# Moving where the matmul operands start in SBUF, modulo 512 bytes, in an attention and MLP kernel

## The chip, the cores and the metric

The kernel runs on one core of a Trainium2 chip. The metric is the device time of one execution in microseconds (us); lower is better. The five engines named here are TensorE (PE, with its weight loads shown apart as PEld), VectorE (DVE), ScalarE (ACT), GpSimd (POOL) and SyncE (SP), which issues most transfers.

## What is computed

The input is q, k and v of shape 4 x 8 x 576 x 64 and two weight matrices, w_in (512 x 2048) and w_out (2048 x 512). Attention is the sum of a global part on tokens averaged in fours and a local part in which a token sees the three before and behind it. Its output, 2304 tokens of 512 features, goes through a two-layer network with a softplus between:

```python
def _attn_ref(q, k, v):                      # B, H, S, D = 4, 8, 576, 64; factor = 4
    out_d = sm_attn(q_d, k_d, v_d)           # q_d, k_d, v_d: means over 4 tokens
    out_up = np.repeat(out_d, factor, axis=2)
    mask = np.abs(pos[:, None] - pos[None, :]) < factor
    ...
    return out_up + np.matmul(attn, v)       # attn: softmax of the masked scores

def _moe_ref(x, w_in, w_out):                # x: 2304 x 512
    h = x @ w_in
    g = np.maximum(h, 0.0) + np.log1p(np.exp(-np.abs(h)))
    return (g @ w_out).astype(np.float32)
```

## The kernel before

**The network's two layers.** Tokens are taken in five groups (`NG`): four of 512 and a last one of 256, the short group. The hidden features are taken in 16 slices of 128 (`NF`). For each group g and slice f, `layer1` multiplies the tokens by 128 columns of w_in, softplus follows, and `layer2` multiplies the result by 128 rows of w_out and adds into four accumulators in PSUM, one for each 128 output features. All of this runs with activations as the moving operand, 512 or 256 columns wide, and weights as the stationary operand, 128 x 128.

**Halves.** Every float32 operand is held as two float32r tiles, a high half and a low half: `xh`, `xl` for the tokens, `gh`, `gl` for the softplus, and `wi..h`, `wi..l`, `wo..h`, `wo..l` for the weights. A product is three matmuls: high by high, low by high, high by low. So a block, one `layer1` or one `layer2` of one f, has 4 x 3 = 12 matmuls. They are recorded on L732 (layer 1) and L797 (layer 2), and they alternate in both lines between the high tile, the low tile and the high tile of the activations.

**Weights in two sets.** The weights of f = 0 to 7 are in the tiles of set 0 (wi0h, wi0l, wo0h, wo0l), those of f = 8 to 15 in set 1 (wi1..., wo1...). Below, "first half" and "second half" of w_in or w_out mean these sets. Set 1 is made in a pool (`late`) that takes the place of the tiles of the first batch's attention (`start`).

**Softplus.** Behind a block of layer 1, ScalarE takes Abs (L752), Exp (L755) and Ln (L756), VectorE adds max(h, 0) (L761), GpSimd makes gh (L770) and VectorE makes gl (L778). `layer2` of a slice runs two slices later than its `layer1` (`LAG`), so in the steady state TensorE runs a block of layer 1 of f and a block of layer 2 of f - 2 by turns.

**Attention.** There are 16 units (a batch and two heads each). The first four run ahead of the network, the other twelve are spread between the blocks of the first groups. A unit cuts the stream of blocks at three places: its scores (L418, L481), its transposes (L550) and its products with v (L574, L582). A unit's output goes to `x`, and ScalarE and VectorE make the halves `xh`, `xl` of it (L617, L623, and `fill` at L645, L650).

**Order.** `Plan` orders all instructions when the program is built, from costs and due times written in the code; no time of the chip enters. Its costs don't depend on addresses.

**Places.** A tile pool lays tiles out in a partition in the order in which they are first made, each behind the last. The one pool `pool` holds everything but the first batch's attention and weight set 1. The places that follow from it are given with the change. The matmul of layer 1, whose operands' places change:

```python
nc.tensor.matmul(
    h.t[:, :n], w[:, cc, fs], x.t[:, cc, :n],
    start=(cc == 0 and k == 0), stop=(cc == NCC - 1 and k == 2),
)
```

Of the kernel before, what the change touches and what calls it, by code (L numbers as in the profile page):

```python
# [10 lines left out]
F32 = mybir.dt.float32  # L11
F32R = mybir.dt.float32r
# [5 lines left out]
ALU = mybir.AluOpType  # L18
# [7 lines left out]
P = 128  # L26
# [3 lines left out]
NCC = DM // P  # L30
# [12 lines left out]
GN = 512  # L43
NG = -(-NT // GN)
FB = NF // 2
SCALE = 1.0 / float(D) ** 0.5
NEG = -1000000000.0
EPS = 1e-09
LAG = 2
ON_PE = ()  # L50
TOP_POOL = lambda which, f: False
V_PE = ()
# [13 lines left out]
def cut(b):  # L66
    return (b + 1) * GN - b * S


def gn(g):  # L70
    return min(GN, NT - g * GN)


FIFO = ("h", "t", "gh", "gl", "xh", "xl", "x")
# [177 lines left out]
def kernel(  # L252
# [8 lines left out]
    out: bass.AP,  # L261
):
    nc = tc.nc
    pool = ctx.enter_context(tc.tile_pool(name="pool", bufs=1))
    psum = ctx.enter_context(tc.tile_pool(name="psum", bufs=1, space=PSUM))
    late = ctx.enter_context(ExitStack())
# [6 lines left out]
    op = plan.op  # L273
# [10 lines left out]

    def new_weights(p):
        i = len(wi)
        wi.append([p.tile([P, NCC, FB * P], F32R, name=f"wi{i}{n}") for n in "hl"])
        wo.append([p.tile([P, FB, DM], F32R, name=f"wo{i}{n}") for n in "hl"])

    new_weights(pool)  # L290
    first = start.__enter__()

    def to_late():
        if len(wi) == 1:
            start.__exit__(None, None, None)
            new_weights(late.enter_context(tc.tile_pool(name="late", bufs=1)))

    def buf(tag, shape, bufs, name, dt=F32, home=None):
        home = home or pool
        assert caps.setdefault(tag, bufs) == bufs  # L300
        return Buf(tag, lambda: home.tile(shape, dt, tag=tag, bufs=bufs, name=name))

    def bank(tag, name):
        return Buf(tag, lambda: psum.tile([P, 512], F32, tag=tag, bufs=BANKS[tag], name=name))
# [5 lines left out]

    xh, xl, xs = {}, {}, {}
    for g in range(NG):
        xh[g] = buf("xh", [P, NCC, GN], 2, f"xh{g}", F32R)
        xl[g] = buf("xl", [P, NCC, GN], 2, f"xl{g}", F32R)
    for b in range(B):
        xs[b] = buf("x", [P, NPAIR, S], 1, f"x{b}")
    xparts = {g: [set() for _ in range(NCC)] for g in range(NG)}
# [6 lines left out]
    def attention(u, s):  # L324
# [23 lines left out]
        scale = SCALE / (FACTOR * FACTOR)  # L348
        if u in ON_PE:
            sums = bank("acc", f"sums{u}")  # L350
# [283 lines left out]
    def fill(b):  # L634
        g = b + 1
        n = S - cut(b)
        cost = 0.2 + NCC * n / 960.0
        prio = 2 * NF * b + 1
        src = [(xs[b], p) for p in range(NPAIR)]
        for p in range(NCC):  # L640
            xparts[g][p].add("tail")
        keys = [(p, "tail") for p in range(NCC)]
        op(
            "ACT", cost, prio,
            lambda: nc.scalar.copy(xh[g].t[:, :, :n], xs[b].t[:, :, cut(b) :]),  # L645
            r=src, w=[(xh[g], x) for x in keys],
        )
        op(
            "DVE", cost, prio + 0.5,
            lambda: nc.vector.tensor_tensor(  # L650
                out=xl[g].t[:, :, :n], in0=xs[b].t[:, :, cut(b) :],
                in1=xh[g].t[:, :, :n].bitcast(F32), op=ALU.subtract,
            ),
            r=src + [(xh[g], x) for x in keys], w=[(xl[g], x) for x in keys], port=True,
        )
# [64 lines left out]
    gt, acc = {}, {}  # L720

    def layer1(g, f):
        i = g * NF + f
        h = bank("acc" if g == 0 and 2 <= f < NSPLIT else "h", f"h{g}_{f}")
        n = gn(g)
        fs = slice(f % FB * P, (f % FB + 1) * P)

        def mm(ccs):
            wih, wil = wi[f // FB]
            for cc in ccs:  # L730
                for k, (w, x) in enumerate(((wih, xh[g]), (wih, xl[g]), (wil, xh[g]))):
                    nc.tensor.matmul(  # L732
                        h.t[:, :n], w[:, cc, fs], x.t[:, cc, :n],
                        start=(cc == 0 and k == 0), stop=(cc == NCC - 1 and k == 2),
                    )

        split = [[cc] for cc in range(NCC)] if f < (2 if g else NSPLIT) else [list(range(NCC))]
        for ccs in split:
            xk = [(cc, part) for cc in ccs for part in sorted(xparts[g][cc])]
            op(  # L740
                "PE", 0.23 * 3 * len(ccs) * n / GN, 2 * i + 0.01 * ccs[0], lambda ccs=ccs: mm(ccs),
                r=[("wh", "i", f), ("wl", "i", f)]
                + [(xh[g], k) for k in xk]
                + [(xl[g], k) for k in xk],
                w=[h],
            )
        hh = lambda: h.t[:, :n]
        tt = buf("t", [P, GN], 2, f"t{g}_{f}")
        tv = lambda: tt.t[:, :n]
        c = 0.1 + 0.5 * n / GN  # L750
        pr = 2 * i + 3
        op("ACT", c, pr, lambda: nc.scalar.activation(out=tv(), in_=hh(), func=AF.Abs), r=[h], w=[tt])  # L752

        def expln():
            nc.scalar.activation(out=tv(), in_=tv(), func=AF.Exp, scale=-1.0)  # L755
            nc.scalar.activation(out=tv(), in_=tv(), func=AF.Ln, bias=1.0)  # L756

        op("ACT", 2 * c, pr, expln, w=[tt])
        op(
            "DVE", 0.15 + 0.54 * n / GN, pr,  # L760
            lambda: nc.vector.scalar_tensor_tensor(  # L761
                out=tv(), in0=hh(), scalar=0.0, in1=tv(), op0=ALU.max, op1=ALU.add
            ),
            r=[h], w=[tt],
        )
        gh = buf("gh", [P, GN], 2, f"gh{g}_{f}", F32R)
        gl = buf("gl", [P, GN], 2, f"gl{g}_{f}", F32R)
        op(
            "POOL", 0.1 + 0.75 * n / GN, pr,
            lambda: nc.gpsimd.tensor_scalar(  # L770
                out=gh.t[:, :n], in0=tv(), scalar1=1.0, scalar2=0.0, op0=ALU.mult, op1=ALU.add
            ),
            r=[tt], w=[gh],
        )
        ge = GL_ENG(g)
        op(
            ge, (1.4 if ge == "POOL" else 0.7) * n / GN, pr,
            lambda: eng[ge].tensor_tensor(  # L778
                out=gl.t[:, :n], in0=tv(), in1=gh.t[:, :n].bitcast(F32), op=ALU.subtract
            ),  # L780
            r=[tt, gh], w=[gl], port=True,
        )
        gt[g, f] = (gh, gl)

    def layer2(g, f):
        i = g * NF + f
        n = gn(g)
        if f == 0:
            acc[g] = [bank("acc", f"acc{g}_{k}") for k in range(NCC)]
        gh, gl = gt.pop((g, f))  # L790

        def mm():
            woh, wol = wo[f // FB]
            for m in range(NCC):
                ms = slice(m * P, (m + 1) * P)
                for k, (w, a) in enumerate(((woh, gh), (woh, gl), (wol, gh))):
                    nc.tensor.matmul(  # L797
                        acc[g][m].t[:, :n], w[:, f % FB, ms], a.t[:, :n],
                        start=(f == 0 and k == 0), stop=(f == NF - 1 and k == 2),
                    )  # L800

        op(
            "PE", 0.23 * 12 * n / GN, 2 * i + 2 * LAG + 1, mm,
            r=[gh, gl, ("wh", "o", f), ("wl", "o", f)], w=acc[g],
        )
        if f < NF - 1:
            return
        final = g == NG - 1
        for m in range(NCC):
            o = buf("stage", [P, 2, GN], 4, f"osb{g}_{m}") if m % 2 == 0 else o  # L810
            e = "ACT" if m % 2 == 0 else "DVE"

            def copy(m=m, o=o):
                d = o.t[:, m % 2, :n]
                if final and m == NCC - 1:
                    nc.vector.tensor_copy(d[:, : n // 2], acc[g][m].t[:, : n // 2])
                    nc.scalar.copy(d[:, n // 2 :], acc[g][m].t[:, n // 2 : n])
                elif m % 2 == 0:
                    nc.scalar.copy(d, acc[g][m].t[:, :n])
                else:  # L820
                    nc.vector.tensor_copy(d, acc[g][m].t[:, :n])

            pr = 2 * i + 2 * LAG + 1
            op(e, 0.65, pr, copy, r=[acc[g][m]], w=[(o, m % 2)])
            q = "ACT" if final and m == NCC - 1 else "SP"

            def store(m=m, o=o, q=q):
                eng[q].dma_start(
                    out=out[m * P : (m + 1) * P, g * GN : g * GN + n], in_=o.t[:, m % 2, :n]
                )  # L830

            op(q, 0.1, pr, store, r=[(o, m % 2)], kb=256)
# [7 lines left out]
    for i in range(P // HW):  # L840
        bm = base[i * HW : (i + 1) * HW, :]
        nc.gpsimd.affine_select(
            out=bm, in_=bm, pattern=[[1, HW]], base=0,
# [3 lines left out]
            out=bm, in_=bm, pattern=[[-1, HW]], base=2 * REACH,  # L847
# [20 lines left out]
    for g in range(NG):  # L868
        for f in range(NF):
            layer1(g, f)  # L870
            i = g * NF + f
            if i >= LAG:
                layer2(*divmod(i - LAG, NF))
    for i in range(NG * NF - LAG, NG * NF):
        layer2(*divmod(i, NF))
# [59 lines left out]
```

## Time and profile before

| | before |
|---|---|
| median of 3 runs | 507.99 us (506.65 to 508.0) |
| span of the profiled execution | 506.7 us |
| TensorE busy (matmuls) | 493.6 us, 97% |
| VectorE busy | 269.2 us, 53% |
| ScalarE busy | 245.2 us, 48% |
| GpSimd busy | 92.0 us, 18% |
| granted TensorE clock, mean | 0.997 of full speed |

The span runs from the first to the last instruction of one execution; what lies around it is not in the profile. A matmul's duration in the profile runs from its start to the modelled end of its results, and the next matmul starts before that end. So durations of matmuls overlap, and how fast a stream of them goes is read from start to start: two rows of the timeline some matmuls apart, divided by their number. The timeline gives starts to 0.01 us, so a step is the better known the more matmuls lie between the two rows.

### The profile page before, as it was taken

Reading aid. Unit: us, or ns where it says so; the run is one execution under the profiler, and the core shown is the slowest. Engines: PE = TensorE matmul, PEld = TensorE weight load, DVE = VectorE, ACT = ScalarE, POOL = GpSimd, SP = SyncE. Lnnn points to the kernel's source line nnn. Section 1 sums busy time; section 2 is a strip of 40 time slices with the busy share of each in tenths; the row PEclk is TensorE's granted clock in tenths of the full one; section 3 lists DMA queues with packets and bytes.
Section 4 is the critical chain, followed back from the end, with each engine's and each line's share of the span. In section 5 each row is a group of like instructions: output and inputs, shape, how many; then the busy total and the mean of one; then the engine's idle time right before and its main releaser. Section 6 shows DMA issues by size and latency. Waiting matters only on the chain.

```text
span 506.7 us, 12503 instructions
## 1 busy us (share of the span) xinstructions
PE 493.6 (97%) x5388; PEld 406.3 (80%) x5388; DVE 269.2 (53%) x512; ACT 245.2 (48%) x528; POOL 92.0 (18%) x133
## 2 busy tenths in 40 slices
PE   6799999999999999999999999999999999999996
PEld 4568778888888888888888888888888888889996
DVE  5667998898877646374264636453332222223322
ACT  3457987678556345333344535342442332234342
POOL 5633131131111111020011201120011001001110
PEclk9989999999999999999999999999999999999999
DMA  8924566666614303021014121100020000002001
GB/s 261 329 70 157 183 217 219 226 180 197 215 34 149 87 1 104 9 97 37 19 50 138 49 56 50 34 1 1 0 84 0 1 1 0 1 0 85 1 1 41
DMA packets 15798, 42.86 MB, mean 85 GB/s; under 512 B 1792, under 2 KB 2304, under 8 KB 15744
## 3 DMA queue, kind: packets, MB, share of 16 engines
q1 hardware_dynamic: 15600, 41.94, 25.8%
q8 instruction: 42, 0.69, 0.6%
q10 hardware_dynamic: 144, 0.13, 0.1%
q14 instruction: 12, 0.10, 0.1%
HBM read 37.35 MB, written 4.72 MB: 83 GB/s over the span
## 4 chain that ended last, share of the span: by engine, by line
PE 95%; DMA 2%; DVE 1%; issue 1%; ACT 0%
PE acc L797 40%; PE h L732 38%; PE po L582 5%; PE psc L481 3%; PE psd L418 3%; PE busy L888 2%; PE po L574 2%; PE pdt L550 2%; DMA wri<-in_w_in_dram 1%; DMA qT<-in_qt_dram 1%; DVE qd L381 0%; DVE kd L381 0%; DVE wri L686 0%; PE psc L474 0%; ACT top L679 0%
## 5 line engine op out<-in xcount | busy, mean ns | idle before, releaser
L761 DVE SCALAR_TENSOR_TENSOR t<-h,t 128x512 f32<-128x512 f32 (+1 forms) x80 | 50.8, 634 | 139.7 <-ACT t L756 139.7
L752 ACT ACTIVATE t<-h 128x512 f32<-128x512 f32 (+1 forms) x80 | 44.4, 555 | 160.6 <-PE h L732 147.1
L770 POOL TENSOR_SCALAR gh<-t 128x512 fp32r<-128x512 f32 (+1 forms) x80 | 51.0, 638 | 345.4 <-PE acc L797 206.7
L778 DVE TENSOR_TENSOR gl<-t,gh 128x512 fp32r<-128x512 f32 (+1 forms) x80 | 52.4, 656 | 42.8 <-POOL gh L770 42.8
L732 PE MATMUL h<-xh,wi0h 128*128 128x512 f32 (+1 forms) x160 | 61.1, 382 | 0.7 <-DVE t L761 0.7
L797 PE MATMUL acc<-gh,wo0h 128*128 128x512 f32 (+1 forms) x160 | 60.1, 376 | 0.0
L732 PE MATMUL h<-xh,wi1h 128*128 128x512 f32 (+1 forms) x160 | 60.1, 376 | 0.0
L797 PE MATMUL acc<-gh,wo1h 128*128 128x512 f32 (+1 forms) x160 | 60.1, 375 | 0.0
L732 PE MATMUL h<-xh,wi0l 128*128 128x512 f32 (+1 forms) x160 | 59.5, 372 | 0.0
L797 PE MATMUL acc<-gl,wo1h 128*128 128x512 f32 (+1 forms) x160 | 59.5, 372 | 0.0
L732 PE MATMUL h<-xl,wi0h 128*128 128x512 f32 (+1 forms) x160 | 59.4, 372 | 0.0
L797 PE MATMUL acc<-gh,wo1l 128*128 128x512 f32 (+1 forms) x160 | 59.4, 371 | 0.0
L732 PE MATMUL h<-xh,wi1l 128*128 128x512 f32 (+1 forms) x160 | 59.4, 371 | 0.0
L732 PE MATMUL h<-xl,wi1h 128*128 128x512 f32 (+1 forms) x160 | 59.3, 371 | 0.0
L797 PE MATMUL acc<-gl,wo0h 128*128 128x512 f32 (+1 forms) x160 | 59.1, 369 | 0.0
L797 PE MATMUL acc<-gh,wo0l 128*128 128x512 f32 (+1 forms) x160 | 59.0, 369 | 0.0
L756 ACT ACTIVATE t<-t 128x512 f32<-128x512 f32 (+1 forms) x80 | 47.2, 590 | 2.5
L755 ACT ACTIVATE t<-t 128x512 f32<-128x512 f32 (+1 forms) x80 | 47.2, 590 | 2.3
L732 PEld LDWEIGHTS h<-xh,wi0h 128*128 128x128 f32 x160 | 30.0, 188 | 6.9 <-DVE t L761 1.4
L732 PEld LDWEIGHTS h<-xh,wi0l 128*128 128x128 f32 x160 | 30.0, 188 | 6.0 <-DVE wi0l L711 0.3
L732 PEld LDWEIGHTS h<-xh,wi1l 128*128 128x128 f32 x160 | 30.1, 188 | 5.7
L797 PEld LDWEIGHTS acc<-gh,wo1l 128*128 128x128 f32 x160 | 30.0, 188 | 5.7
(90 smaller groups left out, 765.0 us busy)
## 6 DMA issues: line engine op xcount, KB each, us to landing
wri<-in_w_in_dram SPq DMA_DIRECT2D x16, 511.8 KB, 6.0
wro<-in_w_out_dram SPq DMA_DIRECT2D x16, 511.8 KB, 4.0
vw<-in_vwin_dram SPq DMA_DIRECT2D x16, 384.0 KB
qT<-in_qt_dram SPq DMA_DIRECT2D x16, 292.0 KB, 3.5
kT<-in_kt_dram SPq DMA_DIRECT2D x16, 292.0 KB, 6.5
stage<-in_vrow_dram SPq DMA_DIRECT2D x16, 288.0 KB
out_dram<-osb SPq DMA_DIRECT2D x16, 256.0 KB, 3.0
out_dram<-osb SPq DMA_DIRECT2D x3, 128.0 KB, 1.8
```

Of the source, the lines that this page charges most:

```text
L418: nc.tensor.matmul(pd3()[:, r, :], qb[:, r * RD : (r + 1) * RD], kd.t, start=True, stop=True)
L481: nc.tensor.matmul(pc()[o : o + HW, t, :], q.t[hp, c : c + HW], k.t[hp, c : c + HW], start=not early, stop=not early or t == NTL - 1,)
L550: nc.tensor.transpose(pt.t[:HD, r * RD : (r + 1) * RD], sd.t[:, r, c * HD : (c + 1) * HD], ident[:RD, :RD],)
L582: nc.tensor.matmul(po[h].t[j * D : (j + 1) * D, t * HT : (t + 1) * HT], vw.t[kp, t, :], sT.t[kp, t, :HT], start=True, stop=True,)
L732: nc.tensor.matmul(h.t[:, :n], w[:, cc, fs], x.t[:, cc, :n], start=(cc == 0 and k == 0), stop=(cc == NCC - 1 and k == 2),)
L752: op("ACT", c, pr, lambda: nc.scalar.activation(out=tv(), in_=hh(), func=AF.Abs), r=[h], w=[tt])
L755: nc.scalar.activation(out=tv(), in_=tv(), func=AF.Exp, scale=-1.0)
L756: nc.scalar.activation(out=tv(), in_=tv(), func=AF.Ln, bias=1.0)
L761: lambda: nc.vector.scalar_tensor_tensor(out=tv(), in0=hh(), scalar=0.0, in1=tv(), op0=ALU.max, op1=ALU.add),
L770: lambda: nc.gpsimd.tensor_scalar(out=gh.t[:, :n], in0=tv(), scalar1=1.0, scalar2=0.0, op0=ALU.mult, op1=ALU.add),
L778: lambda: eng[ge].tensor_tensor(out=gl.t[:, :n], in0=tv(), in1=gh.t[:, :n].bitcast(F32), op=ALU.subtract),
L797: nc.tensor.matmul(acc[g][m].t[:, :n], w[:, f % FB, ms], a.t[:, :n], start=(f == 0 and k == 0), stop=(f == NF - 1 and k == 2),)
```

## The change

A new pool, `even`, is opened ahead of `pool`. A pad of 96 float32 is its first tile, and xh, xl, gh and gl are made in it. A pad is also made ahead of each set of weights (32 and 112 float32). The columns of the short group start at column 240 (960 bytes) of their buffers instead of column 0: in `fill`, which writes xh and xl, in the two instructions that write gh and gl, and in the matmuls of both layers (`cols`).

The rows of a tile are multiples of 512 bytes apart in these operands, so one number, the place modulo 512, holds for all slices of a tile:

| start in the partition, modulo 512 bytes | before | after |
|---|---|---|
| xh, xl (moving, layer 1) | 192 | 0 |
| gh, gl (moving, layer 2) | 0 | 0 |
| wi0, wo0 (first half of the weights) | 256 | 256 |
| wi1, wo1 (second half) | 320 | 256 |
| moving columns of the short group, layer 1 | 192 | 448 |
| moving columns of the short group, layer 2 | 0 | 448 |

From the moving tile's start to the weight tile's start, modulo 512, this is:

| distance in bytes, modulo 512 | before | after |
|---|---|---|
| layer 1, first half of w_in | 64 | 256 |
| layer 1, second half | 128 | 256 |
| layer 2, first half of w_out | 256 | 256 |
| layer 2, second half | 320 | 256 |
| short group, all four kinds | 64, 128, 256, 320 | 320 |

In whole addresses, xh, xl, gh and gl move from 107,200 to 156,672 bytes to 1,536 to 42,496, ahead of everything else; weight set 0 moves from 7,936 to 49,408, and set 1 from 162,112 to 163,072. Of the other tiles, ident, mask, the block tile of the later units and the tiles of the weights' upper parts (`top`) change their place modulo 512 by 128 bytes, and so do some small tiles of sums; q, k, v, the staging tiles, t and attention's other tiles keep theirs.

The order of the instructions is the same, row for row, on every engine; only addresses differ.

```diff
--- before.py
+++ after.py
@@ -47,6 +47,9 @@
 NEG = -1000000000.0
 EPS = 1e-09
 LAG = 2
+EVEN_PAD = 96
+ODD_PAD = (32, 112)
+SHORT_AT = 240
 ON_PE = ()
 TOP_POOL = lambda which, f: False
 V_PE = ()
@@ -69,6 +72,11 @@
 
 def gn(g):
     return min(GN, NT - g * GN)
+
+
+def cols(g):
+    o = 0 if gn(g) == GN else SHORT_AT
+    return slice(o, o + gn(g))
 
 
 FIFO = ("h", "t", "gh", "gl", "xh", "xl", "x")
@@ -261,6 +269,8 @@
     out: bass.AP,
 ):
     nc = tc.nc
+    even = ctx.enter_context(tc.tile_pool(name="even", bufs=1))
+    even.tile([P, EVEN_PAD], F32, name="evenpad")
     pool = ctx.enter_context(tc.tile_pool(name="pool", bufs=1))
     psum = ctx.enter_context(tc.tile_pool(name="psum", bufs=1, space=PSUM))
     late = ctx.enter_context(ExitStack())
@@ -284,6 +294,7 @@
 
     def new_weights(p):
         i = len(wi)
+        p.tile([P, ODD_PAD[i]], F32, name=f"oddpad{i}")
         wi.append([p.tile([P, NCC, FB * P], F32R, name=f"wi{i}{n}") for n in "hl"])
         wo.append([p.tile([P, FB, DM], F32R, name=f"wo{i}{n}") for n in "hl"])
 
@@ -310,8 +321,8 @@
 
     xh, xl, xs = {}, {}, {}
     for g in range(NG):
-        xh[g] = buf("xh", [P, NCC, GN], 2, f"xh{g}", F32R)
-        xl[g] = buf("xl", [P, NCC, GN], 2, f"xl{g}", F32R)
+        xh[g] = buf("xh", [P, NCC, GN], 2, f"xh{g}", F32R, even)
+        xl[g] = buf("xl", [P, NCC, GN], 2, f"xl{g}", F32R, even)
     for b in range(B):
         xs[b] = buf("x", [P, NPAIR, S], 1, f"x{b}")
     xparts = {g: [set() for _ in range(NCC)] for g in range(NG)}
@@ -635,6 +646,7 @@
         g = b + 1
         n = S - cut(b)
         cost = 0.2 + NCC * n / 960.0
+        gc = slice(cols(g).start, cols(g).start + n)
         prio = 2 * NF * b + 1
         src = [(xs[b], p) for p in range(NPAIR)]
         for p in range(NCC):
@@ -642,14 +654,14 @@
         keys = [(p, "tail") for p in range(NCC)]
         op(
             "ACT", cost, prio,
-            lambda: nc.scalar.copy(xh[g].t[:, :, :n], xs[b].t[:, :, cut(b) :]),
+            lambda: nc.scalar.copy(xh[g].t[:, :, gc], xs[b].t[:, :, cut(b) :]),
             r=src, w=[(xh[g], x) for x in keys],
         )
         op(
             "DVE", cost, prio + 0.5,
             lambda: nc.vector.tensor_tensor(
-                out=xl[g].t[:, :, :n], in0=xs[b].t[:, :, cut(b) :],
-                in1=xh[g].t[:, :, :n].bitcast(F32), op=ALU.subtract,
+                out=xl[g].t[:, :, gc], in0=xs[b].t[:, :, cut(b) :],
+                in1=xh[g].t[:, :, gc].bitcast(F32), op=ALU.subtract,
             ),
             r=src + [(xh[g], x) for x in keys], w=[(xl[g], x) for x in keys], port=True,
         )
@@ -730,7 +742,7 @@
             for cc in ccs:
                 for k, (w, x) in enumerate(((wih, xh[g]), (wih, xl[g]), (wil, xh[g]))):
                     nc.tensor.matmul(
-                        h.t[:, :n], w[:, cc, fs], x.t[:, cc, :n],
+                        h.t[:, :n], w[:, cc, fs], x.t[:, cc, cols(g)],
                         start=(cc == 0 and k == 0), stop=(cc == NCC - 1 and k == 2),
                     )
 
@@ -763,12 +775,12 @@
             ),
             r=[h], w=[tt],
         )
-        gh = buf("gh", [P, GN], 2, f"gh{g}_{f}", F32R)
-        gl = buf("gl", [P, GN], 2, f"gl{g}_{f}", F32R)
+        gh = buf("gh", [P, GN], 2, f"gh{g}_{f}", F32R, even)
+        gl = buf("gl", [P, GN], 2, f"gl{g}_{f}", F32R, even)
         op(
             "POOL", 0.1 + 0.75 * n / GN, pr,
             lambda: nc.gpsimd.tensor_scalar(
-                out=gh.t[:, :n], in0=tv(), scalar1=1.0, scalar2=0.0, op0=ALU.mult, op1=ALU.add
+                out=gh.t[:, cols(g)], in0=tv(), scalar1=1.0, scalar2=0.0, op0=ALU.mult, op1=ALU.add
             ),
             r=[tt], w=[gh],
         )
@@ -776,7 +788,7 @@
         op(
             ge, (1.4 if ge == "POOL" else 0.7) * n / GN, pr,
             lambda: eng[ge].tensor_tensor(
-                out=gl.t[:, :n], in0=tv(), in1=gh.t[:, :n].bitcast(F32), op=ALU.subtract
+                out=gl.t[:, cols(g)], in0=tv(), in1=gh.t[:, cols(g)].bitcast(F32), op=ALU.subtract
             ),
             r=[tt, gh], w=[gl], port=True,
         )
@@ -795,7 +807,7 @@
                 ms = slice(m * P, (m + 1) * P)
                 for k, (w, a) in enumerate(((woh, gh), (woh, gl), (wol, gh))):
                     nc.tensor.matmul(
-                        acc[g][m].t[:, :n], w[:, f % FB, ms], a.t[:, :n],
+                        acc[g][m].t[:, :n], w[:, f % FB, ms], a.t[:, cols(g)],
                         start=(f == 0 and k == 0), stop=(f == NF - 1 and k == 2),
                     )
```

## Rows read from the trace of the kernel before

**Rows 1.** The page: TensorE's busy time, share, instructions; the last chain's shares by engine
```profile
PE 493.6 (97%) x5388; PEld 406.3 (80%) x5388; DVE 269.2 (53%) x512; ACT 245.2 (48%) x528; POOL 92.0 (18%) x133
...
PE 95%; DMA 2%; DVE 1%; issue 1%; ACT 0%
```

**Rows 2.** Groups by line, forms apart, TensorE: operation, shape, count | busy, ns of one
```profile
L732 PE MATMUL h<-xh,wi0h 128*128 128x512 f32 x128 | 52.1, 407 | 0.7 <-DVE t L761 0.7
...
L418 PE MATMUL psd<-kd,block 128*96 128x144 f32 x96 | 15.2, 297 | 0.0
...
L550 PE MATMUL pdt<-ident,sd 96*72 96x96 f32 x96 | 11.5, 252 | 1.1 <-issue 1.1
...
L797 PE MATMUL acc<-gh,wo0l 128*128 128x256 f32 x32 | 9.0, 282 | 0.0
```

**Rows 3.** Timeline, TensorE: start, us, line, tiles; layer 2, first half, undisturbed
```profile
61.34 0.39 PE L797 MATMUL acc<-gl,wo0h 128*128 128x512 f32 x1
...
65.42 0.39 PE L797 MATMUL acc<-gl,wo0h 128*128 128x512 f32 x1
```

**Rows 4.** Timeline, TensorE: block of layer 2, then of layer 1, first halves
```profile
387.94 0.39 PE L797 MATMUL acc<-gh,wo0h 128*128 128x512 f32 x1
...
389.32 0.39 PE L797 MATMUL acc<-gh,wo0h 128*128 128x512 f32 x1
...
390.68 0.39 PE L732 MATMUL h<-xh,wi0h 128*128 128x512 f32 x1
...
393.48 0.39 PE L797 MATMUL acc<-gh,wo0h 128*128 128x512 f32 x1
```

**Rows 5.** Timeline, TensorE: block of layer 1, then of layer 2, second halves
```profile
423.95 0.39 PE L732 MATMUL h<-xh,wi1h 128*128 128x512 f32 x1
...
426.73 0.39 PE L797 MATMUL acc<-gh,wo1h 128*128 128x512 f32 x1
...
429.52 0.39 PE L732 MATMUL h<-xh,wi1h 128*128 128x512 f32 x1
```

**Rows 6.** Timeline, TensorE: layer 2, first half, behind a piece of attention
```profile
280.84 0.50 PE L797 MATMUL acc<-gh,wo0h 128*128 128x512 f32 x1
281.18 0.39 PE L797 MATMUL acc<-gl,wo0h 128*128 128x512 f32 x1
...
283.48 0.39 PE L797 MATMUL acc<-gh,wo0l 128*128 128x512 f32 x1
```

**Rows 7.** Timeline, TensorE: the one wait in layer 1 [idle before, who ended it]
```profile
57.38 0.50 PE L732 MATMUL h<-xh,wi0h 128*128 128x512 f32 x1 [0.69 <-DVE t L761]
```

**Rows 8.** Timeline, TensorE: short group, blocks with first halves, then second halves
```profile
468.68 0.29 PE L732 MATMUL h<-xh,wi0h 128*128 128x256 f32 x1
...
470.06 0.28 PE L797 MATMUL acc<-gh,wo0h 128*128 128x256 f32 x1
...
470.52 0.28 PE L797 MATMUL acc<-gl,wo0h 128*128 128x256 f32 x1
...
471.48 0.29 PE L732 MATMUL h<-xh,wi0h 128*128 128x256 f32 x1
...
484.20 0.28 PE L797 MATMUL acc<-gh,wo1h 128*128 128x256 f32 x1
...
485.56 0.28 PE L732 MATMUL h<-xh,wi1h 128*128 128x256 f32 x1
...
486.99 0.28 PE L797 MATMUL acc<-gh,wo1h 128*128 128x256 f32 x1
```

**Rows 9.** Windows: 55 to 130 us; busy us (x instructions) by engine
```profile
55.00:130.00 75.00, 74.31 (x772) 59.71 (x771) 66.29 (x116) 60.39 (x115) 17.37 (x15) 1.00 0.61 198
```

**Rows 10.** Timeline, VectorE, TensorE, weight load: gl of the short group, and its readers
```profile
486.77 0.43 DVE L778 TENSOR_TENSOR gl<-t,gh 128x256 fp32r<-128x256 f32 x1 [0.62 <-POOL gh L770]
...
489.92 0.28 PE L797 MATMUL acc<-gl,wo1h 128*128 128x256 f32 x1
...
501.29 0.19 PEld L797 LDWEIGHTS acc<-gl,wo1h 128*128 128x128 f32 x1 [0.22 <-DVE gl L778]
```

## The prediction

> **What bounds the kernel now.** I read the page first. TensorE is busy for 493.6 us of a span of 506.7 us and holds 95% of the chain that ended last [rows 1], so only what shortens or lengthens TensorE's stream moves the time. The groups by line, with forms kept apart, say what that stream is [rows 2]: twelve groups of 128 matmuls of 512 columns (1536) and twelve of 32 matmuls of 256 columns (384), six of each on L732 (layer 1) and six on L797 (layer 2); one row of each width is shown. The 0.40 us and 0.28 us that these rows give as the duration of one are not what a matmul costs, because the next one starts before the last has left. The cost is the step from one start to the next, so I went to the timeline of TensorE and took starts.
>
> The steps are not alike, though every matmul has the same shape. Layer 2 with the first half of w_out runs from 61.34 to 65.42 us in 18 steps, 226.7 ns each [rows 3]. Where no attention work interferes, a layer-2 block of 12 with that same half takes 2.74 us: its first six steps 1.38 us and its last six 1.36 us, which is again 226.7 ns; the block of layer 1 behind it, with the first half of w_in, takes 2.80 us, 233.3 ns a step [rows 4]. With the second halves, layer 1 takes 2.78 us and layer 2 takes 2.79 us [rows 5]. The order of work is the same in all four and no wait stands in these rows. What differs is the distance in bytes, modulo 512, from the moving tile's start to the weight tile's start: 256 in the fast case, 64 (layer 1, first half), 128 (layer 1, second half) and 320 (layer 2, second half) in the others. The profile doesn't show a mechanism; it shows that the step goes with the pair of operands and that the fast pair needs some steps to settle.
>
> **The change part by part.** No instruction is added, removed or moved on any engine; tiles move. All 512-column pairs get the distance 256, the fast one. The columns of the short group start 960 bytes into their buffers, so its distance is 256 - 960, which is 320 modulo 512.
>
> Full groups. If each pair behaves as layer 2 with the first half does now, a block of 12 takes 12 x 226.7 ns = 2.72 us. There are four full groups of 16 blocks for each layer, 8 of them with each half. Per group this gives 8 x (2.80 - 2.72) + 8 x (2.78 - 2.72) + 8 x (2.74 - 2.72) + 8 x (2.79 - 2.72) = 0.64 + 0.48 + 0.16 + 0.56 = 1.84 us, and 7.4 us for four groups.
>
> What comes off that. The settled step has to be found again after each piece of attention. Row group 6 shows one such place: the first matmul behind the scores takes 0.34 us, and the next ten steps, 281.18 to 283.48, take 2.30 us, 0.03 to 0.04 us over ten settled ones [rows 6]. Twelve units of attention lie in the stream of the full groups and each cuts it at three places (scores, transposes, values), so 36 x 0.04 = 1.4 us. The 36 first steps themselves (0.34 us) I leave as they are: 36 x 0.005 = 0.2 us of the sum is not gained. And TensorE waits once in layer 1, 0.69 us before 57.38 us, for VectorE [rows 7]; about four blocks of layer 1 lie ahead of that wait, and what they gain, 4 x 0.08 = 0.3 us, only lengthens it. Full groups: 7.4 - 1.4 - 0.2 - 0.3 = 5.5 us.
>
> Short group. Its four kinds of block take 1.38 us (layer 1, first half), 1.42 (layer 2, first), 1.43 (layer 1, second) and 1.36 (layer 2, second) now [rows 8]. The last is the one with distance 320, and 1.36 / 12 = 113.3 ns a step. After the change all four have that distance, though with both operands 64 bytes lower, modulo 512, than the pair that shows it now. If only the distance counts, the gain is 8 x (0.02 + 0.06 + 0.07 + 0) = 1.2 us. If the absolute place counts too, the nearest slow row is the settled 120 ns of layer 2 with the first half (470.52 to 471.48 us, eight steps) [rows 8]: all 384 at 120 ns would be 46.1 us against 8 x (1.38 + 1.42 + 1.43 + 1.36) = 44.7 us now, a loss of 1.4 us. I take the gain, because the row with that very distance has it, and keep both ends.
>
> Attention and the rest. The staging tiles, q, k, v and most of attention's tiles keep their place modulo 512; ident, mask, the late block tile and the two top tiles move by 128 bytes. Of the matmuls late in the stream that touches L418 (block) and L550 (ident), 15.2 and 11.5 us busy [rows 2]. The widest difference between the full-width steps is 233.3 against 226.7, 3%; 3% of 26.7 us is 0.8 us, up or down. Nothing says which way, so I take 0 and keep 0.8 us for the range. ScalarE, VectorE and GpSimd do the same work at other addresses; they are not on the chain, and the wait below is what they could cost.
>
> Cover. A faster TensorE asks for its inputs sooner. From 55 to 130 us VectorE is busy for 66.29 of 75 us [rows 9], the tightest stretch; if everything TensorE gains there were given back in new waits, 27 blocks x 0.06 = 1.6 us would be lost. In the short group a gl tile is ready at 486.77 + 0.43 = 487.20 us and is first read at 489.92, 2.7 us later [rows 10], against a gain of about 0.09 us in each pair of blocks; no wait arises there. At the end TensorE waits 0.22 us for the last gl tile [rows 10]; the 24 matmuls between the last layer-1 block and it have 113.3 ns steps already, so that wait stays as it is.
>
> Sum: 5.5 + 1.2 = 6.7 us. The profiled execution has a span of 506.7 us; the median of the runs is 507.99 us, 1.3 us more, which is about their own scatter (506.65 to 508.0). I take that difference as unchanged: 508.0 - 6.7 = 501.3 us.
>
> **A rule that speaks against it.** The rows above show one shape of matmul at 226.7 and at 233.3 ns, by which weights it loads beside [rows 3, 4]. The Trainium skill, page "TensorE: Matmul & The Clock Gate", section "Step-by-step: what each phase is for", says that TensorE has two separate read ports into SBUF, one for the stream and one for the weights, so that loading the next weights takes nothing from the running matmul. By that rule the place of a tile can't matter, the change is worth 0, and the time stays at 508.0 us. The trace speaks against the rule as far as the steps differ; it can't show that the place is the reason, since place, layer and half go together in it.
>
> **Rivals.**
> 1. *The place does nothing.* The steps differ for another reason that goes with the layer and the half. For it: no pair appears at two distances in this trace, and layer 1 differs from layer 2 in more than its offset. Against: the 12 matmuls alternate the same way in both, and the first and second half of one layer have the same code. Time: 508.0 us. This is also the case that the skill's rule gives.
> 2. *Only layer 2 follows.* Layer 1 streams x, whose four column blocks lie 2048 bytes apart and whose two halves lie 16,384 bytes apart in the new layout; the fast row is layer 2 alone, with gh and gl 4096 bytes apart. Then layer 1 stays at 2.80 and 2.78 us and interrupts each layer-2 block, which doesn't settle before its seventh step: layer 2's second half falls from 2.79 to 2.74 us, 32 x 0.05 = 1.6 us, and the short group gives its 1.2 us. Time: about 505.2 us.
> 3. *The pairs settle on a slow step (slower than before).* A pair can hold more than one pace: the short group's first-half pair in layer 2 settles at 120 ns [rows 8], while the full-width pair at that same distance settles at 226.7 ns, nearer to 113.3 per 256 columns. Now a boundary between two distances comes every 12 matmuls and throws out whatever pace was reached; with one distance throughout, a slow pace would never be thrown out. At 233.3 ns (2.80 us) the 128 full blocks, which take (2.80 + 2.74 + 2.78 + 2.79) / 4 = 2.78 us on average, cost 128 x 0.02 = 2.9 us more, and the short group 1.4 us more. Time: 512.3 us. It decides from a settled step of 2.78 / 12 = 231.5 ns upward. Against it: in both stretches where the pair at 256 ran on, it went to 226.7 ns and stayed there [rows 3, 4].
> 4. *VectorE becomes the bound from 55 to 130 us.* Price 1.6 us, time about 502.9 us; it lies inside the forecast's own range.
>
> **How the numbers follow.** My forecast, with rival 4 in it, gets 0.69 (0.62 of it without waits), at 501.3 us with its own range of 499 to 503.5: the upper end has VectorE's waits and a short group without a gain, the lower end has breaks that cost nothing (1.6 us) and attention's 0.8 us. Rival 2 gets 0.12, rival 1 gets 0.12, rival 3 gets 0.07. The range for 8 in 10 takes in rival 2 and leaves the other two out: 499.0 to 505.5 us. A measurement of this kernel tells about 0.3% (1.5 us) from no change, so faster is 0.69 + 0.12 = 0.81, same 0.12, slower 0.07.
>
> **What would show it.** In the profile of the changed kernel, blocks of 12 in an undisturbed stretch should begin 2.72 us apart in both layers and with both halves, and 1.36 us apart in the short group. Layer 1 at 2.78 us or more with layer 2 at 2.74 means rival 2; all four as today, rival 1; 2.80 us throughout, rival 3. Waits of TensorE for VectorE between 55 and 130 us mean rival 4. The groups of the other engines should keep their durations. I am wrong at the root if the steps are equal in all pairs but not 226.7 ns, or if they follow the layer and not the distance.

## The result, and the profile after

The changed kernel takes 500.21 us (median of 6 runs, 498.79 to 502.2) against 507.13 us (504.52 to 508.0): the ratio to the kernel before is 0.9879, 95% interval 0.9854 to 0.9904. That is 6.1 us less by the ratio (4.9 to 7.4 us); the two medians lie 6.9 us apart. The forecast was 501.3 us. A second comparison on another occasion gave 0.9887 (0.9859 to 0.9915). The span of the profiled execution went from 506.7 to 500.4 us.

The page of the changed kernel, the lines that answer to [rows 1]. TensorE is still the chain.

```profile
PE 489.1 (98%) x5388; PEld 407.0 (81%) x5388; DVE 269.3 (54%) x512; ACT 245.0 (49%) x528; POOL 92.6 (19%) x133
...
PE 96%; DVE 1%; ACT 1%; DMA 1%; issue 0%
```

Timeline of TensorE (start, duration, line, tiles), undisturbed stretches of the changed kernel: a block of layer 1 and one of layer 2 with the first halves, then one of layer 2 and one of layer 1 with the second halves, then a block of layer 2 behind a piece of attention, then one of layer 1 in the short group, and the one wait in layer 1.

```profile
380.24 0.39 PE L744 MATMUL h<-xh,wi0h 128*128 128x512 f32 x1
...
382.96 0.39 PE L809 MATMUL acc<-gh,wo0h 128*128 128x512 f32 x1
...
385.68 0.39 PE L744 MATMUL h<-xh,wi0h 128*128 128x512 f32 x1
...
421.04 0.39 PE L809 MATMUL acc<-gh,wo1h 128*128 128x512 f32 x1
...
423.76 0.39 PE L744 MATMUL h<-xh,wi1h 128*128 128x512 f32 x1
...
426.48 0.39 PE L809 MATMUL acc<-gh,wo1h 128*128 128x512 f32 x1
...
277.98 0.40 PE L809 MATMUL acc<-gl,wo0h 128*128 128x512 f32 x1
...
280.27 0.39 PE L809 MATMUL acc<-gh,wo0l 128*128 128x512 f32 x1
...
465.10 0.28 PE L744 MATMUL h<-xh,wi0h 128*128 128x256 f32 x1
...
466.51 0.28 PE L809 MATMUL acc<-gh,wo0h 128*128 128x256 f32 x1
...
56.58 0.50 PE L744 MATMUL h<-xh,wi0h 128*128 128x512 f32 x1 [0.67 <-DVE t L773]
```

All four kinds of full-width block take 2.72 us, where [rows 4, 5] had 2.80, 2.74, 2.78 and 2.79. Behind attention ten steps take 2.29 us, as [rows 6] had 2.30. The short block takes 1.41 us, 117.7 ns a step: not the 1.36 us that was forecast. The wait ahead of 56.58 us is 0.67 us, where [rows 7] had 0.69.

Adding up every step from start to start that is shorter than 0.26 us at full width and 0.13 us in the short group, the full groups have 1481 steps of 231.8 ns on average in the trace before and 1481 of 227.4 ns in a second trace of the changed kernel (1479 of 227.5 in the first): 6.4 us less. The short group has 381 steps of 117.2 ns before and 117.7 ns after: 0.2 us more. Together that is 6.2 us less, inside the interval of the ratio.

### The profile page after: what moved, and what is told of

It reads as the page before. It is cut to its first block, busy times and chain, and to the rows that moved or that the text cites. A ratio compares the mean times of both kernels' runs of the same rounds, so it can differ in the third digit from the quotient of the medians.

```text
span 500.4 us, 12503 instructions
## 1 busy us (share of the span) xinstructions
PE 489.1 (98%) x5388; PEld 407.0 (81%) x5388; DVE 269.3 (54%) x512; ACT 245.0 (49%) x528; POOL 92.6 (19%) x133
## 4 chain that ended last, share of the span: by engine, by line
PE 96%; DVE 1%; ACT 1%; DMA 1%; issue 0%
PE acc L809 40%; PE h L744 39%; PE po L593 5%; PE psc L492 3%; PE busy L900 3%; PE psd L429 3%; PE po L585 2%; PE pdt L561 2%; DMA qT<-in_qt_dram 1%; DVE qd L392 0%; DVE kd L392 0%; DVE wo0l L723 0%; PE psc L485 0%; DVE t L773 0%; DVE wri L698 0%
## 5 line engine op out<-in xcount | busy, mean ns | idle before, releaser
L809 PEld LDWEIGHTS acc<-gl,wo1h 128*128 128x128 f32 x160 | 30.1, 188 | 5.3 <-DVE gl L790 0.5
L809 PEld LDWEIGHTS acc<-gh,wo0l 128*128 128x128 f32 x160 | 30.2, 189 | 5.1
```

The lines of the kernel that those rows point to most:

```text
L809: nc.tensor.matmul(acc[g][m].t[:, :n], w[:, f % FB, ms], a.t[:, cols(g)], start=(f == 0 and k == 0), stop=(f == NF - 1 and k == 2),)
```

## The experiments

In all of them the order of the instructions is that of the changed kernel; only places differ. "Distance" is, as ahead, from the moving tile's start to the weight tile's, modulo 512. Diffs are against the changed kernel unless a heading says otherwise. The theories: **D**, the distance sets the step; **P**, each operand's own place does; **L**, the layer does. For the short group, once its forecast had failed: **M**, at one distance the stream can hold one of two paces, and how it was entered decides which; **N**, the distance alone decides.

### Everything 64 bytes further

```diff
-EVEN_PAD = 96
+EVEN_PAD = 112
```

> All operands of the two layers are moved 64 bytes further, halves and weights alike: full-width moving at 64, weights at 320, short columns at 0 (modulo 512). Every distance stays as in the changed kernel: 256 for full width, 320 for the short group. Theory D (only the distance counts): full-width steps settle at 226.7 ns as in the changed kernel, short steps at 117.7 ns as there, time about 500 us. Theory P (each operand's absolute place counts): the short pair now stands exactly where layer 2's second half stood before (0 and 320), so its steps go to 113.3 ns as they did there, 1.7 us less, and the full-width steps move off 226.7 ns, toward 231 to 233 ns, 6 us more.

Measured: 499.01 us (one run). Timeline of TensorE, second halves at full width, then the short group, second halves:

```profile
423.36 0.39 PE L809 MATMUL acc<-gh,wo1h 128*128 128x512 f32 x1
...
426.08 0.39 PE L744 MATMUL h<-xh,wi1h 128*128 128x512 f32 x1
...
428.80 0.39 PE L809 MATMUL acc<-gh,wo1h 128*128 128x512 f32 x1
...
471.87 0.28 PE L809 MATMUL acc<-gh,wo0h 128*128 128x256 f32 x1
...
473.28 0.28 PE L744 MATMUL h<-xh,wi1h 128*128 128x256 f32 x1
```

Full-width blocks stay at 2.72 us in both layers although every operand moved. That is D, and P falls. The short blocks stay at 1.41 us, although their operands now stand exactly (0 and 320) where layer 2's second half stood when it took 1.36 us [rows 8]. So the absolute place doesn't explain the failed term either.

### The halves of x and softplus alone

```diff
-ODD_PAD = (32, 112)
-SHORT_AT = 240
+ODD_PAD = (32, 128)
+SHORT_AT = 0
```

> Only the first part of the change: xh, xl, gh, gl at 0 modulo 512; weights of the first half at 256 and of the second half at 320 as before the change; short columns at 0. Theory D: full-width blocks at distance 256 (first half) settle at 226.7 ns in both layers, blocks at 320 (second half) take 2.79 us in both layers. Against the changed kernel 64 blocks x (2.79 - 2.72) = 4.5 us more; the short group by its pace at 256 and 320, 120 ns and 113.3 ns, 192 x 2.3 - 192 x 4.4 ns = 0.4 us less; time about 504.3 us. Rival L (layer 1 gains by x's move whatever the weights): second half of layer 1 stays near 2.72 us, time about 502 us.

Measured: 505.22 us against 505.87 us before, ratio 0.9995 (0.9982 to 1.0009): this part alone can't be told from no change. Timeline of TensorE, a block of layer 1 with the first half, then one of each layer with the second halves:

```profile
386.11 0.39 PE L744 MATMUL h<-xh,wi0h 128*128 128x512 f32 x1
...
388.83 0.39 PE L809 MATMUL acc<-gh,wo0h 128*128 128x512 f32 x1
...
419.12 0.40 PE L744 MATMUL h<-xh,wi1h 128*128 128x512 f32 x1
...
421.92 0.40 PE L809 MATMUL acc<-gh,wo1h 128*128 128x512 f32 x1
...
424.72 0.40 PE L744 MATMUL h<-xh,wi1h 128*128 128x512 f32 x1
```

At 256 layer 1 takes 2.72 us; at 320 both layers take 2.80 us. So L falls: with the second half of w_in, layer 1 lost 0.02 us a block by this move. Nor is it the move to the front of the partition, in whole addresses, that makes the blocks fast: this run has it too. The short group took 118.7 ns a step on average, 0.4 us more than in the changed kernel, where 0.4 us less was expected: at 320 it kept 117.7 ns here too. In the stream the part is worth 1.0 us (full groups 1.6 us less, short group 0.6 us more, both against the kernel before).

### The second half of the weights alone, on the kernel before

```diff
         i = len(wi)
+        if i:
+            p.tile([P, 112], F32, name="oddpad")
```

> The kernel before with only the second half of the weights moved, from 320 to 256 modulo 512; xh and xl stay at 192, gh and gl at 0, the short columns at column 0. Distances: 64 in layer 1 and 256 in layer 2, both halves. Theory D, with the steps of earlier traces: layer 1 takes 2.80 us a block in both halves (32 blocks 0.02 us dearer than before), layer 2 2.74 us in both, since each block starts anew behind one at 64 (32 blocks 0.05 us cheaper): 1.0 us less than before. With x's move alone giving about 1.6 us in the full groups, the two alone would then give 2.6 us of the 6.0 us that they give together. If settling across blocks doesn't matter, layer 2 goes to 2.72 us in all its blocks and w_only gives 2.2 us.

Measured: 505.73 us (one run), before 505.77; a single run can't show 1.0 us, the steps of its trace can. Timeline of TensorE, second halves, a block of layer 1 and one of layer 2:

```profile
421.60 0.39 PE L734 MATMUL h<-xh,wi1h 128*128 128x512 f32 x1
...
424.39 0.39 PE L799 MATMUL acc<-gh,wo1h 128*128 128x512 f32 x1
...
427.13 0.39 PE L734 MATMUL h<-xh,wi1h 128*128 128x512 f32 x1
```

Layer 2 at 256 takes 2.74 us when a block at 64 lies ahead of each, not 2.72: it has to settle anew in every block. The full-width steps average 231.1 ns against 231.8, so 1481 of them give 1.0 us. The two parts alone give 1.6 and 1.0 us in the full groups, 2.6 us of the 6.4 us that they give together. The rest, 3.8 us, comes only with both. Most of it, 2.8 us, is layer 1's second half: x's move alone takes its distance from 128 to 320, the weights' move alone takes it to 64, and only both together take it to 256. Its steps average 231.8 ns before, 233.3 ns with either part and 227.2 ns with both. Most of what remains, 0.8 us, is layer 2's second half, which at 256 averages 228.8 ns between slow blocks and 227.3 ns when all blocks are alike.

### Layer 2 at layer 1's old distances

```diff
-ODD_PAD = (32, 112)
-SHORT_AT = 240
+ODD_PAD = (112, 0)
+SHORT_AT = 0
```

> xh, xl, gh, gl at 0, short columns at 0, weights of the first half at 64 and of the second half at 128 modulo 512: distances 64 and 128 in both layers and both widths. Before the change layer 1 alone had these. Theory D: layer 2 now takes layer 1's old blocks, 2.80 us (first half) and about 2.78 us (second half) in both layers: against the changed kernel 64 x 0.08 + 64 x 0.06 = 9 us more, less 1.6 us of settling that no longer matters, about 507 to 509 us. Rival L: layer 2 keeps 2.74 us or less with the first half, 502 to 505 us.

Measured: 507.20 us (one run). Timeline of TensorE, a block of layer 2 with the first half, then two starts six blocks apart with the second halves:

```profile
386.85 0.39 PE L809 MATMUL acc<-gh,wo0h 128*128 128x512 f32 x1
...
389.65 0.39 PE L744 MATMUL h<-xh,wi0h 128*128 128x512 f32 x1
...
420.40 0.40 PE L809 MATMUL acc<-gh,wo1h 128*128 128x512 f32 x1
...
437.13 0.39 PE L809 MATMUL acc<-gh,wo1h 128*128 128x512 f32 x1
```

At 64 layer 2 takes layer 1's old 2.80 us, and at 128 six blocks take 16.73 us, 2.79 us each. L falls a second time, and this is the price of rival 3 at full width: a stream that settles on 233.3 ns and stays there. It is 7 to 8 us slower than the changed kernel's 499 to 500 us, where 9 less 1.6 was expected.

### Distances 0 and 192, then 384 and 448

```diff
-ODD_PAD = (32, 112)
-SHORT_AT = 240
+ODD_PAD = (96, 32)
+SHORT_AT = 0
```

> xh, xl, gh, gl at 0, short columns at 0, weights of the first half at 0 and of the second half at 192 modulo 512: distances 0 and 192, which no kernel had so far. Theory D says that both layers show the same step at one distance and says nothing of its size: the four full-width distances seen (64, 128, 256, 320) gave 226.7 to 233.3 ns, so 1536 x 226.7 to 1536 x 240 ns, 499 to 520 us. Rival P or L: the two layers differ at one distance.

Measured: 501.68 us (one run). Timeline of TensorE: starts two blocks apart at distance 0, then six apart at 192, then four blocks of the short group:

```profile
384.86 0.39 PE L744 MATMUL h<-xh,wi0h 128*128 128x512 f32 x1
...
390.30 0.39 PE L744 MATMUL h<-xh,wi0h 128*128 128x512 f32 x1
...
420.35 0.39 PE L809 MATMUL acc<-gh,wo1h 128*128 128x512 f32 x1
...
436.83 0.39 PE L809 MATMUL acc<-gh,wo1h 128*128 128x512 f32 x1
...
473.59 0.28 PE L744 MATMUL h<-xh,wi1h 128*128 128x256 f32 x1
...
475.00 0.28 PE L809 MATMUL acc<-gh,wo0h 128*128 128x256 f32 x1
...
476.43 0.28 PE L744 MATMUL h<-xh,wi1h 128*128 128x256 f32 x1
...
477.79 0.28 PE L809 MATMUL acc<-gh,wo1h 128*128 128x256 f32 x1
```

Distance 0 gives 5.44 us for two blocks, 2.72 each, just as 256 does. Distance 192 gives 16.48 / 6 = 2.75 us. In the short group, layer 1 with the second half, at 192, takes 1.41 us from 473.59 and 1.36 us from 476.43, with a block of layer 2 at distance 0 between: one pair, one distance, two paces in one trace.

```diff
-ODD_PAD = (32, 112)
-SHORT_AT = 240
+ODD_PAD = (64, 128)
+SHORT_AT = 0
```

> Moving operands at 0, weights of the first half at 384 and of the second half at 448 modulo 512, short columns at 0. If distances 256 apart are the same (theory M), 384 is 128 again with full-width steps of 232.3 ns on average in both layers, and 448 is 192 with 229.0 ns: 1481 steps at 230.7 ns, 5 us more than the changed kernel. If the period is 512, other values at either.

Measured: 505.63 us (one run). Timeline of TensorE: starts five blocks apart at 384, then six apart at 448:

```profile
384.81 0.39 PE L809 MATMUL acc<-gh,wo0h 128*128 128x512 f32 x1
...
398.81 0.39 PE L744 MATMUL h<-xh,wi0h 128*128 128x512 f32 x1
...
421.00 0.39 PE L744 MATMUL h<-xh,wi1h 128*128 128x512 f32 x1
...
437.48 0.39 PE L744 MATMUL h<-xh,wi1h 128*128 128x512 f32 x1
```

14.00 / 5 = 2.80 us at 384 is near 128's 2.79, and 16.48 / 6 = 2.75 us at 448 is 192's. With 0 and 256 at 2.72 and 64 and 320 at 2.80, four pairs of distances 256 apart agree to 0.01 us: as far as these show, the step repeats every 256 bytes, not every 512.

### Distances off the grid of 64 bytes

```diff
-ODD_PAD = (32, 112)
-SHORT_AT = 240
+ODD_PAD = (104, 160)
+SHORT_AT = 0
```

> Moving operands at 0, weights of the first half at 32 modulo 512, of the second half at 224 modulo 256, short columns at 0: distances 32 and 224, half of the 64-byte grid that all kernels so far stand on. Theory G (the step goes with the distance in pieces of 64 bytes): each shows the settled steps of a neighbour on the grid, 226.7 or 233.3 ns at 32 and 226.7 or 229 ns at 224. Otherwise another step shows, which no run has given a value for: between 220 and 240 ns, 490 to 520 us.

Measured: 508.82 us (one run). Timeline of TensorE: starts five blocks apart at 32, then six apart at 224:

```profile
384.69 0.40 PE L744 MATMUL h<-xh,wi0h 128*128 128x512 f32 x1
...
398.69 0.40 PE L809 MATMUL acc<-gh,wo0h 128*128 128x512 f32 x1
...
421.08 0.39 PE L809 MATMUL acc<-gh,wo1h 128*128 128x512 f32 x1
...
437.88 0.39 PE L809 MATMUL acc<-gh,wo1h 128*128 128x512 f32 x1
```

Both give 2.80 us a block, although 224 lies between 192 (2.75) and 256 (2.72). It is 32 bytes from the fast distance on either side that costs the full price; between these distances the step does not change gradually. No distance that was tried is below 2.72 us. 16 bytes and less, and the distances between 64 and 192 other than 128, were not tried.

### The short group at 64 and at 192

```diff
-SHORT_AT = 240
+SHORT_AT = 48
```

> The changed kernel with the short group's columns at column 48 (192 bytes) instead of 240: short distance 64 instead of 320, full width untouched at 256. The steps seen at 64 in the short group were 113.3 ns throughout where both layers had it and the stream came from distance 128. Theory M (distances 256 apart are the same, and at one distance the short steps have two paces, 113.3 and 117.7 ns, chosen by the pace before): 64 is 320 again and the stream comes from the same settled 226.7 ns, so the steps stay at 117.7 ns, change of time 0. Theory N (64 is a better distance than 320): 113.3 ns, 381 x 4.4 ns = 1.7 us less.

```diff
-SHORT_AT = 240
+SHORT_AT = 16
```

> The changed kernel with the short group's columns at column 16 (64 bytes): short distance 192, full width untouched at 256. With both layers at 192 behind distance 0 the short steps went to 113.3 ns after four blocks at 117.7. Theory M: which of the two paces is reached depends on how it is entered, so 113.3 or 117.7 ns, no value between; at 113.3 ns 1.7 us less than the changed kernel. Theory N (the distance alone): 113.3 ns from the first blocks on.

Measured: 499.64 and 499.33 us (one run each). Timeline of TensorE, one short block of the first, and of the second:

```profile
473.87 0.28 PE L744 MATMUL h<-xh,wi1h 128*128 128x256 f32 x1
...
475.28 0.28 PE L809 MATMUL acc<-gh,wo1h 128*128 128x256 f32 x1
```

```profile
473.54 0.28 PE L744 MATMUL h<-xh,wi1h 128*128 128x256 f32 x1
...
474.95 0.28 PE L809 MATMUL acc<-gh,wo1h 128*128 128x256 f32 x1
```

Both hold 1.41 us, and the steps of the whole short group average 117.7 and 117.8 ns. N falls: 64 gave 113.3 ns in the experiment with layer 2 at 64, and 192 gave it in the last part of its own. Here the short steps come out of a stream settled at 226.7 ns and keep 117.7 ns. (The four blocks that the second expectation mentions were two at 192, at about 117.7 ns a step, and two at 0, at 119 to 120 ns.)

### One block at 128 in the short group

The softplus halves of the short group's first slice start at column 32, so one block of layer 2 has distance 128; all other short blocks keep 320.

```diff
+KICK = (0,)
+KICK_AT = 32
+def gcols(g, f):
+    c = cols(g)
+    if gn(g) < GN and f in KICK:
+        c = slice(KICK_AT, KICK_AT + gn(g))
+    return c
...
-                out=gl.t[:, cols(g)], in0=tv(), in1=gh.t[:, cols(g)].bitcast(F32), op=ALU.subtract
+                out=gl.t[:, gcols(g, f)], in0=tv(), in1=gh.t[:, gcols(g, f)].bitcast(F32), op=ALU.subtract
...
-                        acc[g][m].t[:, :n], w[:, f % FB, ms], a.t[:, cols(g)],
+                        acc[g][m].t[:, :n], w[:, f % FB, ms], a.t[:, gcols(g, f)],
```

> The changed kernel, except that the softplus halves of the short group's first slice start at column 32 (128 bytes) instead of 240: one block of layer 2 has distance 128, all other short blocks keep 320. Theory M (two paces at distance 320, chosen by how it is entered): 117.7 ns in the blocks ahead of that one block, another pace behind it, 113.3 ns as before the change, where each block at 320 came behind one at 128; then about 1.4 us less than the changed kernel. Theory P (the place 448 or 256 itself makes 117.7 ns): 117.7 ns ahead of it and behind it, change of time 0.

Measured: 500.15 us (one run) and, in the short group, 43.5 us for 381 steps against 44.9. The time of that run doesn't show the gain; its wait for VectorE in layer 1 was 2.0 us, where the changed kernel's was 0.7. The kernel was then timed, beside the changed kernel on one chip:

> The changed kernel with one block of layer 2 of the short group at distance 128. Theory M: short steps of 113.3 ns behind that block as in its first trace, 44.9 - 43.5 = 1.4 us less than the changed kernel, ratio to before about 0.985 to 0.986. If the pace is reached by chance of the run and not by that block: short steps of 117.7 ns again and the ratio of the changed kernel.

> The changed kernel itself, for a comparison with the next kernel on one chip. Theory D with the steps of its first trace: full-width steps 227.5 ns on average and short steps 117.8 ns, 6.0 us less than before in the full groups and 0.2 us more in the short one: ratio to before about 0.988.

Measured: 498.08 us (497.16 to 499.01, 5 runs), ratio to before 0.9841 (0.9822 to 0.9860); the changed kernel 499.94 us (498.42 to 503.81, 6 runs), ratio 0.9887 (0.9859 to 0.9915). Timeline of TensorE in the timed kernel's trace: a block of layer 1 ahead of the block at 128, that block, the next of layer 2 at 320, and then three blocks by turns:

```profile
453.26 0.28 PE L753 MATMUL h<-xh,wi0h 128*128 128x256 f32 x1
...
454.67 0.28 PE L818 MATMUL acc<-gh,wo0h 128*128 128x256 f32 x1
...
456.11 0.28 PE L818 MATMUL acc<-gh,wo0h 128*128 128x256 f32 x1
...
457.48 0.28 PE L753 MATMUL h<-xh,wi0h 128*128 128x256 f32 x1
...
458.84 0.28 PE L818 MATMUL acc<-gh,wo0h 128*128 128x256 f32 x1
...
460.20 0.28 PE L753 MATMUL h<-xh,wi0h 128*128 128x256 f32 x1
```

The block ahead takes 1.41 us, the one at 128 takes 1.44, the next, which settles, 1.37, and every one behind it 1.36 us. The pace of 113.3 ns came in both traces of this kernel and in none of the five others in which all short blocks had one distance (320 three times, 64, 192) behind a settled stream. That is what M expected. But M doesn't say which neighbour moves the stream, and that stays open: in the run with the halves alone two blocks at 256 stood between the first blocks at 320, and those at 320 kept 1.41 to 1.42 us. The gain of 1.4 us by the traces is less than the two intervals can tell apart; as a ratio to before, this version is the best measured.

## Why the prediction was right, and where it was not

**Bound.** Right. TensorE's starts are the time, and reading steps from start to start, not durations, was what made the four kinds of block visible: the mean duration in the first group only went from 407 ns [rows 2] to 404 ns.

**Full groups, 5.5 us.** The mechanism was right and shown by the shift of 64 bytes and the layer-2 test; the settled 2.72 us came in all four kinds of block. Measured 6.4 us. The difference is in what was taken off: the mean of 227.4 ns lies 0.8 ns over the settled 226.7, so settling costs 1481 x 0.0008 = 1.2 us after the change, near the 1.4 us forecast, but the kernel before paid for its cuts too, and the sum, made from undisturbed blocks alone, left that out: 231.8 ns over all steps against 2.7775 / 12 = 231.5 ns in the blocks of [rows 4, 5], 0.4 us. The 0.3 us taken off for the wait didn't show either: what the blocks ahead of it gained should have lengthened it from 0.69 to 1.0 us, and it was 0.67 us, and 0.8 in the second trace of the changed kernel.

**Short group, 1.2 us.** This step failed: it came out 0.2 us slower. The step said "if only the distance counts" and took the row at distance 320 [rows 8] for what that distance gives. The uniform shift shows that distance and place were both reproduced and the 113.3 ns didn't come; the single block at 128 shows what was missing. Before the change each block at 320 but the last came behind one at 128 and ended at the fast pace; in the changed kernel the short blocks come straight from the settled full-width stream and hold 117.7 ns. The row taken was also the fastest of its kind. Five of the eight blocks at 320 took 1.39 us, of which the first six steps took 0.71 us and the last six 0.68 us, which is 113.3 ns a step; the kernel before, a block of layer 2 with the second half:

```profile
486.99 0.28 PE L797 MATMUL acc<-gh,wo1h 128*128 128x256 f32 x1
...
487.70 0.28 PE L797 MATMUL acc<-gh,wo1h 128*128 128x256 f32 x1
...
488.38 0.28 PE L732 MATMUL h<-xh,wi1h 128*128 128x256 f32 x1
```

So the trace before already showed that this pair has to settle and that its step hangs on what ran ahead. The price of the wrong choice, 1.4 us, was inside the range.

**Sum, 6.7 us.** The steps gave 6.2 us. The full groups gave 0.9 us more than forecast and the short group 1.4 us less, so that the total came this close is partly luck. The base moved as well: 501.3 us was reckoned from a median of 507.99 us, and with more runs that median is 507.13 us.

**Rivals.** The rule of the Trainium skill (page "TensorE: Matmul & The Clock Gate", section "Step-by-step: what each phase is for"), that loading weights takes nothing from the running matmul, does not hold here as far as time goes: the same matmuls at other distances take 226.7 to 233.3 ns. Why the step grows is not shown by any trace, only that it goes with the relative place of the two operands. With that, rival 1 falls; rival 2 falls by layer 1's 2.72 us in the changed kernel, and again by the experiment on the halves alone. Rival 3's premise, that a pair can hold more than one pace and that boundaries throw it out, was right, and for the short group it is what happened; at full width and distance 256 the stream went back to 226.7 ns each time that it ran on: in the second trace of the changed kernel 12 of 1157 steps beyond the eighth of an uninterrupted stretch are above 230 ns. Rival 4 didn't come: in the changed kernel VectorE is busy for 66.07 of the 75 us, as [rows 9] had 66.29, and TensorE's only wait in layer 1 is the one that was there. The windows view, 55 to 130 us (columns as in [rows 9]):

```profile
55.00:130.00 75.00, 74.26 (x800) 60.35 (x800) 66.07 (x116) 60.24 (x116) 17.39 (x15) 1.00 0.63 198
```

**Attention.** The 0.8 us kept for the range wasn't needed: the two groups of [rows 2] are L429 and L561 in the changed kernel and keep 15.2 and 11.5 us there.

**Median and span.** What lies ahead of the network moves from run to run: the first matmul of layer 1 starts at 43.55 us in the trace before, at 42.87 and 44.90 us in two traces of the changed kernel and at 40.25 us in that of the uniform shift. With that start taken off, the four spans leave 463.1, 457.6, 457.1 and 457.0 us, so it is most of the scatter between these traces, and it is why the steps in the stream tell more here than single times.

## What to carry to other kernels

When a long stream of one matmul shape holds different steps by operand, compare where its two operands start in SBUF relative to each other before anything else; here 32 bytes were worth 3% of a full-width block. Look at every pair before moving one operand, since an operand belongs to several pairs: each part of this change alone moved one kind of block to a slower distance and gave 1.0 to 1.6 us in the full groups, and both gave 6.4. A fast block between slow ones also spends its first steps settling. A step read from one place in a trace belongs to that pair and to what ran ahead of it; before it is carried to another place, see whether the same pair shows a second pace anywhere.

## What the runs showed that was not expected

The step of full-width matmuls repeats with the distance every 256 bytes: 2.72 us a block at 0 and 256, 2.80 at 64 and 320, 2.79 and 2.80 at 128 and 384, 2.75 at 192 and 448, 2.80 at 32 and 224. At 256 columns the stream has two lasting paces at the same distance, 113.3 and 117.7 ns (seen at 64, 192 and 320), and one block of 12 matmuls at another distance was enough to move it from the slow one to the fast one for the rest of the short group, though not every such block does, and what decides it is open.
